# Top-k attention and SwiGLU on one core: scores and V of two units at a time, and the top-k mask applied after Exp

## The chip, the cores and the metric

The kernel runs on one core of a Trainium2 chip. The metric is the time of one execution on the device in microseconds (us). The core has a matrix engine (PE, with its weight loads shown as PEld), a Vector engine (DVE), a Scalar engine (ACT), GpSimd (POOL) and a queue that issues DMAs (SP). They work side by side, each through its own instructions in order, and wait for each other through semaphores.

## The reference

```
# q, k, v: (B=8, H=8, S=576, D=64), all float32
scores = q @ k^T / sqrt(D)
kth    = the 32nd largest score of each row
scores = where(scores >= kth, scores, -1e9)
attn   = exp(scores - max) / (sum + 1e-9)
x      = (attn @ v), brought to (B*S = 4608, H*D = 512)

# FFN: w_gate, w_val (512, 1536), w_out (1536, 512)
g   = x @ w_gate
out = (g * sigmoid(g) * (x @ w_val)) @ w_out        # (4608, 512)
```

## The kernel before, in words

**Attention.** The work is cut into 160 units, `units`: a batch, a query tile (four of 128 queries, a fifth, `qt == J`, of 64) and a pair of heads `hp`. A full unit has both heads side by side: `sc` and `e` hold 128 x 1152 elements, 576 keys for each head. A unit of the fifth tile has the two heads' 64 queries in the two halves of the partitions, and so only 576 columns. The keys are cut into four chunks of 128 (`JP` = 512 keys) and a last one of 64.

One unit goes through these functions:

- `scores(n)` (L308, and L294 for the fifth tile): Q times K into four PSUM tiles of 288 columns (two for the fifth tile). The 64 rows of each head stand in one half of the array's rows, so that two products run side by side in a tiling written 64\*128 in the trace. ACT copies the results to `sc` (L313, L299).
- `select(n)`: DVE finds the 32 largest of each row by four MAX8 (L328), with three MATCH_REPLACE8 between them (L332) that take the found ones out. Then one TENSOR_SCALAR (L338) makes from `sc` the penalty `(sc < kth) * -3e38` in `e`.
- `penalize(n)`: POOL multiplies the largest by the scale for Exp's bias (L348) and adds `sc` to the penalty (L350).
- `weigh(n)`: ACT takes Exp of `e`, with its sum in `tot` (L359, the sum is read by an instruction of its own), and adds eps (L364).
- `normalize(n)`: DVE takes the reciprocal of `tot` (L371), ACT scales `e` by it (L374).
- `turn(n)`: PE transposes `e` in chunks (L386), ACT copies them to `et` (L387).
- `values(n)`: V times `et`. The last keys of both heads stand in one 128 x 128 tile, `vl`, whose other quarters are zero (L406, the whole array, 128\*128); the four other chunks go by pairs of 64 columns, one for each head, side by side (L415, 128\*64). ACT copies the result into `xT`, the FFN's input (L430).

`fetch` (L263, L255) transposes the Q and K of the next batch's head pairs.

**FFN.** 18 blocks of 256 tokens. `feed(kb)` makes the instructions of a block in pieces: 12 products of `x` with a slice of the two weights (L470), each of two pieces of four matmuls; ACT and POOL work on each (gate: L495, L496, L497 and the product L498; value: L502 and L503); then the output product, for all blocks but the first by seven products of quarters (L556) with sums on POOL. A block can start when all its V results are in `xT`; eight units make a block and some of the next.

**Order.** The program writes the order of each engine by hand. The loop at the end has one turn for each unit, and in turn n it puts, each on its engine's queue:

```python
penalize(n - 1); flush(on_pool); run(scaled)     # scaled: unit n - 2's scaling on ACT
finish_unit(n - 3)                               # V
run(nxt); weigh(n - 1)                           # nxt: scores(n + 1)
dve(2); pieces(2); dve(1); dve(1)                # top-k of unit n
run(turn(n - 2)); pieces(1); dve(1); pieces(1); dve(2)
run(topk); next(norm); pieces(6)                 # rest of top-k, reciprocal of n - 1
```

`dve(k)` puts k steps of top-k for each head on DVE; `pieces(k)` puts up to k FFN pieces as long as `credit` allows. What ACT and POOL have to do for the pieces is kept in `on_act` and `on_pool` and put in their queues by `flush`. `share(n)` gives the credit of a turn: 7.0 (6.4 after the first block) pieces for a full unit, half for the fifth tile, less what the turn's scores (0.7), transposes (0.6) and V (0.7) take. In the last four turns it is 8. What is left runs after the loop. `weights()` rounds the FFN's weights during the first turns (L114 to L123).

PSUM has eight banks: five for `ps_t` (scores, transposes, V) and three for `ps_f` (FFN). `sc` and `e` have three buffers each, `et` two.

Of the kernel before, what the change touches and what calls it, by code (L numbers as in the profile page):

```python
# [9 lines left out]
ALU = mybir.AluOpType  # L10
# [15 lines left out]
def kernel(  # L26
# [66 lines left out]
    for i in range(NV):  # L93
        vt = consts.tile([P, P], FP32, name=f"vlast{i}")
        nc.vector.memset(vt[:], 0.0)
        vlast.append(vt)
    eps = consts.tile([P, 1], FP32, name="eps")
    nc.vector.memset(eps[:], EPS)
    wg = consts.tile([P, KC, DFF], FP32, name="wg")
    wv = consts.tile([P, KC, DFF], FP32, name="wv")  # L100
    wo = consts.tile([P, MC, DM], FP32, name="wo")
# [130 lines left out]
    def load_v(i):  # L232
        b, hp = pairs[i]
        h = slice(2 * hp, 2 * hp + 2)
        vt = slabs.tile([P, 2, J, D], FP32, tag="v", name="v")
        v_last = slabs.tile([R, 2, D], FP32, tag="vl", name="v_last")
        vl = vlast[i % NV]
        nc.sync.dma_start(
            vt[:].rearrange("p h j d -> p h (j d)"),
            v[b, h, 0:JP].rearrange("h (p j) d -> p h (j d)", j=J),  # L240
        )
        nc.sync.dma_start(v_last[:], v[b, h, JP:S].rearrange("h p d -> p h d"))
        for hh in range(2):
            o = hh * R
            nc.sync.dma_start(vl[o : o + R, o : o + R], v[b, 2 * hp + hh, JP:S])
        vs[i] = (vt, v_last, vl)
# [27 lines left out]
    def n_heads(qt):  # L274

        return 1 if qt == J else 2
# [39 lines left out]
    def select(n):  # L316

        nh = n_heads(units[n][1])
        sc = state[n]["sc"]
        m = small.tile([P, 2, TOP_K], FP32, tag="m", name="m", bufs=2)  # L320
        heads = [slice(t * S, (t + 1) * S) for t in range(nh)]
        e = work.tile([P, 2 * S], FP32, tag="e", name="e", bufs=3)
        state[n] |= dict(m=m, e=e, heads=heads)
        cur = sc
        rounds = TOP_K // 8
        for r in range(rounds):
            for t, hs in enumerate(heads):
                nc.vector.max(m[:, t, 8 * r : 8 * r + 8], cur[:, hs])  # L328
                yield
            if r < rounds - 1:  # L330
                for t, hs in enumerate(heads):
                    nc.vector.match_replace(  # L332
                        e[:, hs], m[:, t, 8 * r : 8 * r + 8], cur[:, hs], LOWEST
                    )
                    yield
                cur = e
        for t, hs in enumerate(heads):
            nc.vector.tensor_scalar(  # L338
                e[:, hs], sc[:, hs], m[:, t, TOP_K - 1 : TOP_K], FAR, ALU.is_lt, ALU.mult
            )  # L340

    def penalize(n):

        st = state[n]
        sc, m, e, heads = st.pop("sc"), st.pop("m"), st["e"], st["heads"]
        nh = len(heads)
        bias = small.tile([P, 2], FP32, tag="bias", name="bias")
        nc.gpsimd.tensor_scalar_mul(bias[:, 0:nh], m[:, 0:nh, 0], -scale)  # L348
        every = slice(0, nh * S)
        nc.gpsimd.tensor_tensor(e[:, every], e[:, every], sc[:, every], ALU.add)  # L350
        st["bias"] = bias

    def weigh(n):

        st = state[n]
        e, heads, bias = st["e"], st["heads"], st.pop("bias")
        tot = small.tile([P, 2], FP32, tag="tot", name="tot")
        for t, hs in enumerate(heads):
            nc.scalar.activation(  # L359
                e[:, hs], e[:, hs], AF.Exp, bias=bias[:, t : t + 1], scale=scale,  # L360
                accum_out=tot[:, t : t + 1],
            )
        nh = len(heads)
        nc.scalar.activation(tot[:, 0:nh], tot[:, 0:nh], AF.Identity, bias=eps[:])  # L364
        st["tot"] = tot

    def normalize(n):
        st = state[n]
        tot, e, heads = st.pop("tot"), st["e"], st.pop("heads")
        nh = len(heads)  # L370
        nc.vector.reciprocal(tot[:, 0:nh], tot[:, 0:nh])  # L371
        yield
        for t, hs in enumerate(heads):
            nc.scalar.mul(e[:, hs], e[:, hs], tot[:, t : t + 1])  # L374

# [18 lines left out]

    xT, done = {}, {}

    def values(n):

        b, qt, hp = units[n]
        vt, v_last, vl = vs[b * NHP + hp]  # L400
        et = state.pop(n)["et"]
        last = qt == J
        ql = R if last else P
        av = ps_t.tile([P, P], FP32, tag="t", name="av")
        if not last:
            nc.tensor.matmul(av[:], vl[:], et[:, J, :], start=True, stop=False)  # L406
        for c in range(J + 1 if last else J):
            kl = R if c == J else P
            for hh in range(2):
                moving = (  # L410
                    et[0:kl, c, hh * R : (hh + 1) * R]
                    if last
                    else et[:, c + hh * (J + 1), :]
                )
                nc.tensor.matmul(  # L415
                    av[hh * R : (hh + 1) * R, 0:ql],
                    v_last[:, hh, :] if c == J else vt[:, hh, c, :],
                    moving,
                    start=last and c == 0,
                    stop=c == (J if last else J - 1),  # L420
                )
        c0 = b * S + qt * P
        at = c0
        while at < c0 + ql:
            kb = at // BLK
            n_c = min((kb + 1) * BLK, c0 + ql) - at
            if kb not in xT:
                xT[kb] = ffn.tile([P, NHP, BLK], FP32, tag="xT", name="xT", bufs=3)
                done[kb] = 0
            nc.scalar.copy(  # L430
                xT[kb][:, hp, at - kb * BLK : at - kb * BLK + n_c],
                av[:, at - c0 : at - c0 + n_c],
            )
            done[kb] += n_c
            at += n_c

    def store(o, g0, cols=slice(0, DM), queues=(nc.sync,)):
# [241 lines left out]
    def fetch(n):  # L679

        b, qt, hp = units[n]
        i = b * NHP + hp
        if qt == 0:
            yield from prep(i)
        if qt == J and i + NHP < len(pairs):
            load(i + NHP)

    def share(n):


        others = 0.0
        for m, cost in ((n + 1, 0.7), (n - TURN, 0.6), (n - VALUES, 0.7)):
            if m >= 0:
                others += cost * (0.5 if units[m][1] == J else 1)
        if units[n + 2][1] == 0:
            others += 0.6

        beside = 6.4 if T[1] else 7.0
        return beside * n_heads(units[n][1]) / 2 - others

    def pieces(n):
        for _ in range(n):
            if credit[0] >= 1:
                credit[0] -= piece()

    def run(steps):
        for _ in steps:
            pass

    def finish_unit(n):  # L710
        values(n)
        b, qt, hp = units[n]
        if qt == J and b + 1 < B:
            load_v((b + 1) * NHP + hp)

    load(0)
    rounding(2)
# [2 lines left out]
    run(scores(0))  # L720
    early[0]()
    run(fetch(1))
    credit = [0.0]
    no = iter(())
    scaled = no
    TURN, VALUES = 2, 3
    due = [2.0]
    for n in range(NU + VALUES):
        nh = n_heads(units[n][1]) if n < NU else 1
        topk = select(n) if n < NU else no  # L730
        norm = normalize(n - 1) if 0 <= n - 1 < NU else no
        nxt = scores(n + 1) if n + 1 < NU else no
        ahead = fetch(n + 2) if n + 2 < NU else no

        def dve(k, beside=True):

            for _ in range(k * nh):
                next(topk, None)
                due[0] += 5 / 6 if beside else 0
                if due[0] >= 1:  # L740
                    due[0] -= 1
                    rounding(1)

        if n >= NU - NHP:
            credit[0] = 8.0
        else:
            credit[0] = min(credit[0] + share(n), share(n) + 1)
        flush(on_act)
        if 0 <= n - 1 < NU:
            penalize(n - 1)  # L750
        flush(on_pool)
        run(scaled)
        if n >= VALUES:
            finish_unit(n - VALUES)
        run(nxt)
        early[0]()
        if 0 <= n - 1 < NU:
            weigh(n - 1)


        dve(2, beside=False)
        if 2 <= n + 2 < NHP:
            load(n + 2)
        if n < NHP:
            load_v(n)
        pieces(2)
        flush(on_act)
        dve(1)
        dve(1)
        if 0 <= n - TURN < NU:  # L770
            run(turn(n - TURN))

        flush(on_pool)
        next(ahead, None)
        pieces(1)
        next(ahead, None)
        dve(1)
        pieces(1)
        dve(2, beside=False)
        run(topk)  # L780
        next(norm, None)
        scaled = norm
        pieces(6)
    while piece():
        pass
# [48 lines left out]
```

## Time and profile before

| what | us |
|---|---|
| median of 10 runs | 1810.04 (1806.59 to 1812.60) |
| the profiled execution | 1811.92 |
| its span, first to last instruction | 1809.9 |
| PE busy | 1706.0 |
| DVE busy | 1616.7 |
| ACT busy | 1220.9 |
| POOL busy | 1038.8 |
| last mask of top-k on DVE (L338) starts at | 1717.9 |

The busy times are of the whole span. A matmul's length in the trace has its way through the array in it, so lengths overlap: what a matmul costs is read from the start of one to the start of the next. The PE clock that the throttle granted was 0.65 in the mean of the first 130 us and 1.00 from 200 to 1666 us.

### The profile page before, as it was taken

Reading aid. Unit: us, or ns where it says so; the run is one execution under the profiler, and the core shown is the slowest. Engines: PE = TensorE matmul, PEld = TensorE weight load, DVE = VectorE, ACT = ScalarE, POOL = GpSimd, SP = SyncE. Lnnn points to the kernel's source line nnn. Section 1 sums busy time; section 2 is a strip of 40 time slices with the busy share of each in tenths; the row PEclk is TensorE's granted clock in tenths of the full one; section 3 lists DMA queues with packets and bytes.
Section 4 is the critical chain, followed back from the end, with each engine's and each line's share of the span. In section 5 each row is a group of like instructions: output and inputs, shape, how many; then the busy total and the mean of one; then the engine's idle time right before and its main releaser. Section 6 shows DMA issues by size and latency. Waiting matters only on the chain.

```text
span 1809.9 us, 30379 instructions
## 1 busy us (share of the span) xinstructions
PE 1706.0 (94%) x10756; PEld 1403.6 (78%) x10756; DVE 1616.7 (89%) x3372; ACT 1220.9 (67%) x2977; POOL 1038.8 (57%) x930
## 2 busy tenths in 40 slices
PE   4559999899999999999999999999999999999999
PEld 2337678687888778887888878888888878888877
DVE  7999999999999989998999989998999979999400
ACT  6778776676767676767766676766776667676522
POOL 5778666455564646564555646655556544646434
PEclk7659999999999999999999999999999999999989
DMA  7433030001200020000200021000300011000000
GB/s 190 127 103 96 21 86 1 12 2 44 50 12 2 14 71 11 13 1 24 71 13 1 14 60 34 1 12 3 92 1 13 1 40 29 13 1 13 1 12 12
DMA packets 109304, 59.64 MB, mean 33 GB/s; under 512 B 88544, under 2 KB 96992, under 8 KB 109152
## 3 DMA queue, kind: packets, MB, share of 16 engines
q1 hardware_dynamic: 108016, 57.37, 12.2%
q8 instruction: 85, 1.39, 0.3%
q14 instruction: 67, 0.55, 0.1%
q10 hardware_dynamic: 1136, 0.33, 0.1%
HBM read 48.23 MB, written 9.44 MB: 32 GB/s over the span
## 4 chain that ended last, share of the span: by engine, by line
PE 83%; DVE 7%; ACT 6%; POOL 2%; issue 0%; DMA 0%; SPq 0%; ACTq 0%; POOLq 0%
PE f L470 40%; PE x_ps L556 9%; PE av L415 8%; PE s L308 8%; PE y_ps L556 7%; PE etps L386 6%; DVE m L328 3%; DVE e L332 3%; PE s L294 2%; PE av L406 2%; ACT et L387 1%; PE o_ps L516 1%; ACT e L359 1%; DVE e L338 1%; DVE size L121 1%; ACT kqT L268 1%
## 5 line engine op out<-in xcount | busy, mean ns | idle before, releaser
L328 DVE MAX8 m<-e 128x8 f32<-128x576 f32 x864 | 614.3, 746 | 3.3
L350 POOL TENSOR_TENSOR e<-e,sc 128x1152 f32<-128x1152 f32 (+1 forms) x160 | 383.0, 2394 | 86.9 <-DVE tot L371 70.9
L332 DVE MATCH_REPLACE8 e<-m,e 128x576 f32<-128x576 f32 x576 | 423.2, 740 | 0.0
L470 PE MATMUL f<-xT,wg 128*128 128x256 f32 x1728 | 407.2, 384 | 0.9 <-ACT xT L430 0.9
L470 PE MATMUL f<-xT,wv 128*128 128x256 f32 x1728 | 403.4, 382 | 0.0
L470 PEld LDWEIGHTS f<-xT,wg 128*128 128x128 f32 x1728 | 322.2, 191 | 61.7 <-issue 20.1
L470 PEld LDWEIGHTS f<-xT,wv 128*128 128x128 f32 x1728 | 320.6, 190 | 59.6 <-issue 19.9
L498 POOL TENSOR_TENSOR h<-h,half_g 128x512 f32<-128x512 f32 x108 | 137.7, 1275 | 286.0 <-ACT h L497 268.3
L503 POOL TENSOR_TENSOR h<-h,val 128x512 f32<-128x512 f32 x108 | 139.5, 1291 | 190.8 <-ACT val L502 190.5
L359 ACT ACTIVATE e<-e,bias 128x576 f32<-128x576 f32 x288 | 224.7, 795 | 26.6 <-POOL e L350 26.5
L374 ACT ACTIVATE e<-e,tot 128x576 f32<-128x576 f32 x288 | 210.1, 776 | 28.1 <-DVE tot L371 28.1
L387 ACT COPY et<-etps 128x512 f32<-128x512 f32 (+1 forms) x448 | 182.3, 480 | 53.6 <-PE etps L386 52.8
L332 DVE MATCH_REPLACE8 e<-m,sc 128x576 f32<-128x576 f32 x288 | 211.6, 740 | 0.0
L328 DVE MAX8 m<-sc 128x8 f32<-128x576 f32 x288 | 202.5, 739 | 9.2 <-ACT sc L313 9.2
L386 PE MATMUL etps<-ident,e 128*128 128x128 f32 (+1 forms) x1312 | 174.5, 278 | 18.6 <-ACT xT L430 12.8
L386 PEld LDWEIGHTS etps<-ident,e 128*128 128x128 f32 (+1 forms) x1312 | 155.0, 143 | 42.7 <-issue 25.1
L313 ACT COPY sc<-s 128x288 f32<-128x288 f32 x512 | 167.7, 417 | 27.4 <-PE s L308 26.2
L308 PE MATMUL s<-kqT 64*128 64x288 f32 x1024 | 172.0, 457 | 13.5 <-ACT kqT L268 12.7
L338 DVE TENSOR_SCALAR e<-sc,m 128x576 f32<-128x576 f32 x288 | 179.4, 659 | 1.1
L415 PE MATMUL av<-et,v 128*64 128x128 f32 (+1 forms) x2560 | 173.4, 280 | 6.9 <-ACT et L387 6.9
L415 PEld LDWEIGHTS av<-et,v 128*64 128x64 f32 x2560 | 136.1, 143 | 32.0 <-ACT et L387 9.3
L495 ACT ACTIVATE h<-f 128x512 f32<-128x512 f32 x108 | 64.1, 593 | 128.3 <-PE f L470 128.3
(73 smaller groups left out, 2043.9 us busy)
## 6 DMA issues: line engine op xcount, KB each, us to landing
v<-in_v_dram SPq DMA_DIRECT2D x32, 256.0 KB, 3.0
kq_in<-in_k_dram SPq DMA_DIRECT2D x63, 128.0 KB, 2.9
kq_in<-in_q_dram SPq DMA_DIRECT2D x63, 128.0 KB, 3.0
w<-in_moe_w_gate_dram SPq DMA_DIRECT2D x12, 512.0 KB, 3.7
w<-in_moe_w_val_dram SPq DMA_DIRECT2D x12, 512.0 KB, 3.7
w<-in_moe_w_out_dram SPq DMA_DIRECT2D x12, 512.0 KB, 3.6
out_dram<-o SPq DMA_DIRECT2D x38, 128.0 KB, 2.4
out_dram<-o SPq DMA_DIRECT2D x16, 256.0 KB, 2.4
```

The costliest lines, as they stand in the source:

```text
L308: nc.tensor.matmul(ps[:, 0:half], slab[d, q0 : q0 + P], slab[d, k0 : k0 + half])
L328: nc.vector.max(m[:, t, 8 * r : 8 * r + 8], cur[:, hs])
L332: nc.vector.match_replace(e[:, hs], m[:, t, 8 * r : 8 * r + 8], cur[:, hs], LOWEST)
L338: nc.vector.tensor_scalar(e[:, hs], sc[:, hs], m[:, t, TOP_K - 1 : TOP_K], FAR, ALU.is_lt, ALU.mult)
L350: nc.gpsimd.tensor_tensor(e[:, every], e[:, every], sc[:, every], ALU.add)
L359: nc.scalar.activation(e[:, hs], e[:, hs], AF.Exp, bias=bias[:, t : t + 1], scale=scale, accum_out=tot[:, t : t + 1],)
L374: nc.scalar.mul(e[:, hs], e[:, hs], tot[:, t : t + 1])
L386: nc.tensor.transpose(ps[0:kl, c * P : (c + 1) * P], e[:, k0 : k0 + kl], ident[:])
L387: nc.scalar.copy(et[0:kl, c0 : c0 + cn, :], ps[0:kl, 0 : cn * P].rearrange("p (c j) -> p c j", c=cn),)
L415: nc.tensor.matmul(av[hh * R : (hh + 1) * R, 0:ql], v_last[:, hh, :] if c == J else vt[:, hh, c, :], moving, start=last and c == 0, stop=c ...
L470: nc.tensor.matmul(ps[:, i, :], w[:, kc, m * P : (m + 1) * P], x[:, kc, :], start=(kc == 0), stop=(kc == KC - 1),)
L556: nc.tensor.matmul(ps, lhsT, T[i][m], start=m == 0, stop=m == MQ - 1)
```

## The change

- **V of two units in one go.** `values` takes two neighbouring units (two head pairs of one query tile) and puts their results in one PSUM tile of 128 x 2 x 128; one ACT copy takes both. In odd turns n it works on units n-3 and n-2; in even turns there is none.
- **Scores of two units in odd turns.** In an odd turn n, scores(n+1) come first, then V of the two units, then the matmuls of scores(n+2); their copies on ACT stand behind Exp and scaling. `share` counts these costs where they now are.
- **Last keys in column pairs.** The tile `vl` is used in two halves of 64 columns, in the tiling of the other chunks, ahead of them.
- **Exp of the bare scores.** MATCH_REPLACE8 writes to a tile of its own, `rest`. In turn n, ACT takes Exp of unit n's scores without mask (`weigh(n)`), with the bias from the first MAX8 by way of POOL, while DVE is at that unit's top-k. At the end of top-k, DVE multiplies the weights by the mask `sc >= kth` and sums them, in one scalar_tensor_tensor for each head. `penalize`, Exp's own sums and ACT's addition of eps are gone; POOL adds eps.
- **Moved.** POOL's addition of eps for unit n-1 stands near the start of turn n, the reciprocal behind the first MAX8 and MATCH_REPLACE8 of unit n, the scaling behind Exp of unit n. The transposes of unit n-1 are in turn n (before: of n-2). The first loads of Q and K and their transposes come a turn earlier (`fetch(n + 3)`).

```diff
@@ select
+        rest = work.tile([P, 2 * S], FP32, tag="rest", name="rest", bufs=1)
         e = work.tile([P, 2 * S], FP32, tag="e", name="e", bufs=3)
+        tot = small.tile([P, 2], FP32, tag="tot", name="tot")
...
-                        e[:, hs], m[:, t, 8 * r : 8 * r + 8], cur[:, hs], LOWEST
+                        rest[:, hs], m[:, t, 8 * r : 8 * r + 8], cur[:, hs], LOWEST
...
-            nc.vector.tensor_scalar(
-                e[:, hs], sc[:, hs], m[:, t, TOP_K - 1 : TOP_K], FAR, ALU.is_lt, ALU.mult
+            nc.vector.scalar_tensor_tensor(
+                e[:, hs], sc[:, hs], m[:, t, TOP_K - 1 : TOP_K], e[:, hs],
+                ALU.is_ge, ALU.mult, accum_out=tot[:, t : t + 1],
             )
@@ weigh (penalize is taken out, its bias is kept here)
         nc.gpsimd.tensor_scalar_mul(bias[:, 0:nh], m[:, 0:nh, 0], -scale)
-        every = slice(0, nh * S)
-        nc.gpsimd.tensor_tensor(e[:, every], e[:, every], sc[:, every], ALU.add)
...
             nc.scalar.activation(
-                e[:, hs], e[:, hs], AF.Exp, bias=bias[:, t : t + 1], scale=scale,
-                accum_out=tot[:, t : t + 1],
+                e[:, hs], sc[:, hs], AF.Exp, bias=bias[:, t : t + 1], scale=scale
             )
-        nc.scalar.activation(tot[:, 0:nh], tot[:, 0:nh], AF.Identity, bias=eps[:])
@@ normalize
+        nc.gpsimd.tensor_scalar_add(tot[:, 0:nh], tot[:, 0:nh], EPS)
+        yield
         nc.vector.reciprocal(tot[:, 0:nh], tot[:, 0:nh])
-        yield
@@ values
-        av = ps_t.tile([P, P], FP32, tag="t", name="av")
-        if not last:
-            nc.tensor.matmul(av[:], vl[:], et[:, J, :], start=True, stop=False)
+        av = ps_t.tile([P, 2, P], FP32, tag="t", name="av")
+        for i, n in enumerate(ns):
...
+                    if c == J:
+                        weights_, at = (v_last[:, hh, :], d) if last else (vl[:, d], None)
...
-                xT[kb][:, hp, at - kb * BLK : at - kb * BLK + n_c],
-                av[:, at - c0 : at - c0 + n_c],
+                xT[kb][:, hps, at - kb * BLK : at - kb * BLK + n_c],
+                av[:, 0 : len(ns), at - c0 : at - c0 + n_c],
@@ the turn
-        if 0 <= n - 1 < NU:
-            penalize(n - 1)
         flush(on_pool)
-        run(scaled)
-        if n >= VALUES:
-            finish_unit(n - VALUES)
-        run(nxt)
-        early[0]()
-        if 0 <= n - 1 < NU:
-            weigh(n - 1)
-        dve(2, beside=False)
+        next(norm, None)
+        if nxt:
+            run(nxt.pop(0))
+        if valued(n):
+            finish_units(valued(n))
+        if nxt:
+            next(nxt[0])
+        dve(1, beside=False)
+        if n < NU:
+            weigh(n)
+        dve(1, beside=False)
+        run(norm)
+        if nxt:
+            run(nxt.pop())
+        early[0]()
...
-        pieces(2)
+        pieces(2 + (n + 1) % 2)
...
         run(topk)
-        next(norm, None)
-        scaled = norm
         pieces(6)
```

## Prediction

> **What bounds the kernel now.** I read the page's busy times and slices first, then the stretches, the waits, the groups, and the matrix engine (PE) in order of time.
>
> ```profile
> PE 1706.0 (94%) x10756; PEld 1403.6 (78%) x10756; DVE 1616.7 (89%) x3372; ACT 1220.9 (67%) x2977; POOL 1038.8 (57%) x930
> ...
> PE   4559999899999999999999999999999999999999
> ...
> DVE  7999999999999989998999989998999979999400
> ```
>
> Two engines are nearly full. In the first three slices PE is half idle, since no FFN block has its inputs yet, and the Vector engine (DVE) works without a gap. Afterwards both are full, and in the last two slices PE works alone. The stretches give this in us (columns: length, then busy time of PE, PEld, DVE, ACT, POOL, the PE clock, DMA):
>
> ```profile
> 0.00:130.00 130.00, 65.06 (x322) 44.85 (x322) 119.72 (x249) 98.02 (x221) 87.59 (x70) 0.65 0.51 139
> 130.00:200.00 70.00, 65.58 (x374) 53.19 (x375) 70.00 (x132) 62.00 (x140) 62.62 (x48) 0.95 0.27 83
> 200.00:1666.00 1466.00, 1439.39 (x9327) 1189.40 (x9326) 1400.43 (x2940) 1010.23 (x2509) 824.08 (x746) 1.00 0.09 23
> 1666.00:1740.00 74.00, 70.33 (x422) 59.45 (x422) 25.27 (x51) 34.70 (x79) 37.81 (x41) 0.99 0.06 15
> ```
>
> From 200 to 1666 us (where DVE begins unit 156) PE idles 26.6 us and DVE 65.6: PE is the bound, DVE 4.5% behind it. ACT and POOL have room. DVE's idle time is all waiting for work behind PE:
>
> ```profile
> DVE tot L371 <- ACT tot L364: 79.7, 32, 14.4
> ...
> DVE e L332 <- PE etps L386: 25.2, 29, 2.3
> ```
>
> So a saving on PE is worth at most what DVE's idle time allows, and time added to DVE beyond that idle time lengthens the run. ACT's and POOL's savings are worth nothing by themselves.
>
> **The change on PE.** In order of time (start, length, engine, line):
>
> ```profile
> 811.47 0.38 PE L406 MATMUL av<-et,vlast 128*128 128x128 f32 x2
> 811.79 1.09 PE L415 MATMUL av<-et,v 128*64 128x128 f32 x16
> 812.81 1.24 PE L308 MATMUL s<-kqT 64*128 64x288 f32 x8
> 813.98 1.56 PE L556 MATMUL x_ps<-wo,h 128*128 128x256 f32 x6
> 815.38 1.89 PE L470 MATMUL f<-xT,wg 128*128 128x256 f32 x8
> ```
>
> Here "128*64" is the tiling of the array, and starts tell more than lengths. Undisturbed passes start 0.109 us apart at 128 columns (a pair of tiles in one such step), 0.243 at 288, 0.216 at 256. So the steps would take 0.22, 0.87, 0.97 and 1.30 us, and from start to start they take 0.32, 1.02, 1.17 and 1.40: 0.55 us more, for three changes of tiling, 0.18 each. V's last-key product costs two steps of 0.109 whether it is one full matmul or a column pair, so this edit alone is worth nothing; it keeps one tiling through both V products. Counted in the order of PE's instructions, 484 changes of tiling become 322: 162 x 0.18 = 29 us less PE work (zero if the changes only move to places where they cost double). V's product for units 6 and 7 also comes in turn 9, not 10, so FFN starts one 12.3 us turn earlier, of which PE idles some 9.
>
> **ACT and POOL.** ACT loses 288 accumulator reads and 160 additions of eps (61.9 + 37.8 + 9.4 us), and 192 copies of V results become 96 of twice the width. POOL loses the penalty (383.0 us) and gains 160 small additions at the price of its bias rows, some 40. Neither engine is on the path, so I price this at nothing; the cover is their idle time (33% and 43%). Loading two head pairs earlier adds nothing to SP's queue but order.
>
> **The change on DVE.** Its other instructions stay; the mask changes:
>
> ```profile
> L328 DVE MAX8 m<-sc 128x8 f32<-128x576 f32 x288 | 202.5, 739 | 9.2 <-ACT sc L313 9.2
> ...
> L338 DVE TENSOR_SCALAR e<-sc,m 128x576 f32<-128x576 f32 x288 | 179.4, 659 | 1.1
> ```
>
> The old mask reads one tensor. Its median length is 511 ns, its next instruction starts 0.418 us later in the median and 0.585 in the mean; the long ones (up to 2.8 us) coincide with a POOL tensor operation, so 0.167 us a head is contention with POOL. A MAX8 over the same 576 elements starts its successor after 0.66. So the old mask is a two-elements-a-cycle pass: 0.418 where one element a cycle would be 0.60 and a fixed part. The new mask reads scores and weights, masks, multiplies and sums. No row shows it. Nearest below: MAX8's 0.66. Nearest above: 0.418 + 0.30 for the other half of the elements, 0.72. I take 0.70. The sum is read out in an instruction of its own on ACT; on DVE the nearest rows are MATCH_VALUE_LOAD (0.066 from start to start) and the reciprocal (0.075 so, 0.156 long): I take 0.07. Contention I leave at 0.167: the POOL operations that collide are FFN's, which remain; the bounds are 0 and 0.25. Together 0.94 against 0.585, 0.355 more a head; bounds 0.14 (0.66 + 0.066) and 0.54 (0.72 + 0.156 + 0.25).
>
> The Trainium skill (VectorE: DVE Perf Modes, The perf-mode tier table) says that a one-tensor fp32 operation in SBUF runs at two elements a cycle and a two-tensor one at one. That is the reading above. A harsher rule speaks against the change: in Vector Engine (DVE) Microarchitecture Reference, Points that are easy to get wrong, the scalar-tensor-tensor form with two non-bf16 SBUF sources is said to halve throughput. Read as half of one element a cycle, that would add another 0.60 a head and 170 us to the sum below. No row here shows it, and the sum doesn't use it.
>
> **The moved waits.** The reciprocal of unit n-1 moves from the end of DVE's turn n to behind its first four operations, 2.8 us in (1.4 in the half turns with 64 queries). It now waits for POOL's addition of eps, queued behind an FFN product that waits for ACT: gate 1.6 us (L495 to L497), POOL product 1.28, addition 0.25, some 3.3 us with hand-overs after PE's last product. Behind it on DVE stands the rest of top-k; for it waits ACT's scaling, then PE's transposes of the same turn, with two or three FFN pieces (1.73 us each) as cover. In turns 1 to 14, where DVE was the bound, PE began its turn up to 4.4 us ahead of DVE; with a lead of 1 to 2 us full turns don't wait, and half turns wait about 0.5: 32 x 0.5 = 15 us.
>
> **The sum.** Units 0 to 155 hold 284 heads. DVE up to unit 156: first wait 10.3 + busy 1590.1 (119.7 + 70.0 + 1400.4) + 284 x 0.355 = 100.8 + stalls 15 = 1716, where it was 1666; the old idle time, 65.6, is used up. From there PE's backlog decides: it began that turn at 1671.5 and took 138.4 us to the end; by the order of instructions 7.0 us of FFN come earlier, and tiling saves 1: 130. Span 1846, plus 2.0 around it (1811.92 - 1809.9), less 1.9 (the profiled run above the median): **1846 us**, slower by 2.0%. PE's idle time up to there grows by the 50 us of DVE, and by 29 - 7 of its own.
>
> **Rivals.** *The new mask is cheap* (other side): if POOL doesn't hold it up and overheads are least, 0.14 a head is 40 us, and the sum gives 1785. PE's floor lies below: 1809.9 - 29 - 9 = 1772. The point of decision is 64 us, 0.23 a head. For it: POOL has 340 us less work. Against: the old penalty began after the mask it followed, so it never stood in that mask's way. *The short chain stalls every turn*: if PE lags as in the middle of the run (its turn began 4 to 6 us after DVE's), the reciprocal waits in full turns too; 0.5 us in each of 128 more gives 64 us, 1910. Against: with DVE longer, PE gets ahead. *The tiling gain doesn't come*: with DVE the bound it costs nothing, 1847.
>
> **Chances.** DVE the bound, 1818 to 1885: 0.58 (the third rival in it). Cheap mask: 0.25 faster, and 0.05 close to even. Stalls, or a mask at its upper bound (1898): 0.12. The range 1785 to 1895 leaves out parts of the first and last rival; the likeliest case alone is 1818 to 1885. About 0.2% (3.6 us) is what a measurement can tell here: faster 0.25, same 0.05, slower 0.70.
>
> **What would show it.** Right: DVE over 95% busy from 200 us on, the mask with its sum 0.85 us a head or more, PE idling some 70 us more before unit 156, 162 fewer gaps at tiling changes, PE alone for 65 us at the end. Wrong: a mask with successors under 0.80 us later; DVE idle before the reciprocal in most turns; PE without gaps.

## The result, and the profile after

The changed kernel takes **1880.86 us** in the median of 8 runs (1875.95 to 1884.17), the kernel before 1809.62 in the median of 28: the ratio is 1.039, 95% interval 1.038 to 1.040, so 71 us slower. 1846 was predicted. The profiled execution took 1876.91 us, its span is 1875.1.

From the page after (busy times, two of the slices, the chain's shares by engine):

```profile
PE 1706.2 (91%) x11012; PEld 1388.3 (74%) x11012; DVE 1723.8 (92%) x3659; ACT 1135.4 (61%) x2433; POOL 721.2 (38%) x930
...
PE   4458999798999999999999999999999999899989
...
DVE  7999999998999999999999999999999999999520
...
DVE 47%; PE 32%; issue 7%; ACT 6%; POOL 6%; DMA 1%; SPq 1%; DVEq 0%; POOLq 0%; ACTq 0%
```

DVE has 107 us more work than before, ACT 86 less and POOL 318 less. The chain that ended last runs through DVE for 47%; in the kernel before it was PE's:

```profile
PE 83%; DVE 7%; ACT 6%; POOL 2%; issue 0%; DMA 0%; SPq 0%; ACTq 0%; POOLq 0%
```

In tenths both rows are eights and nines nearly throughout; the stretches tell the engines apart (columns as before; unit 156 now begins at 1746 us):

```profile
0.00:130.00 130.00, 61.58 (x356) 43.01 (x356) 116.80 (x252) 91.81 (x189) 62.09 (x68) 0.67 0.51 136
130.00:200.00 70.00, 63.09 (x360) 52.26 (x361) 66.12 (x132) 58.13 (x118) 48.89 (x44) 0.95 0.27 88
200.00:1746.00 1546.00, 1461.01 (x9649) 1190.14 (x9648) 1512.88 (x3223) 947.00 (x2054) 555.92 (x755) 0.99 0.09 22
```

From 200 us to unit 156 DVE is busy 97.9% of the time and PE 94.5%: they have changed places. The new mask in the groups (busy time, mean ns of one, idle before):

```profile
L338 DVE SCALAR_TENSOR_TENSOR e<-sc,m,e 128x576 f32<-128x576 f32 x288 | 291.4, 1043 | 4.3
```

and, in the groups by form, the read-out of its sum:

```profile
L338 DVE DVE_READ_ACCUMULATOR e<-sc,m,e 128x1 f32 x288 | 22.8, 79 | 0.0
```

The old mask's row had 659 ns in the mean. In order of time (start, length, engine), one unit's two masks:

```profile
1292.84 0.82 DVE L338 SCALAR_TENSOR_TENSOR e<-sc,m,e 128x576 f32<-128x576 f32 x1
1293.02 1.77 POOL L493 TENSOR_TENSOR h<-h,half_g 128x512 f32<-128x512 f32 x1 [2.38 <-ACT h L492]
1293.57 0.10 DVE L338 DVE_READ_ACCUMULATOR e<-sc,m,e 128x1 f32 x1
1293.57 1.84 DVE L338 SCALAR_TENSOR_TENSOR e<-sc,m,e 128x576 f32<-128x576 f32 x1
...
1296.88 0.22 POOL L359 TENSOR_SCALAR tot<-tot 128x2 f32<-128x2 f32 x1
...
1298.11 0.15 DVE L361 RECIPROCAL tot<-tot 128x2 f32<-128x2 f32 x1
```

The first mask's successor starts 0.73 us after it, together with the read-out of the sum, which so costs nothing. The second starts while POOL works on an FFN product and takes 1.84. Eps (L359) stands behind that product and the next. Last, what DVE waited for up to unit 156, in the changed kernel (us in total, times, longest):

```profile
DVE tot L361 <- POOL tot L359: 28.2, 20, 4.2
DVE m L328 <- ACT sc L311: 9.2, 1, 9.2
DVE size L119 <- ACT size L112: 3.1, 2, 2.5
DVE vlast L95 <- PEq L828: 0.8, 1, 0.8
```

and the two larger waits of the kernel before, up to its unit 156 (the prediction shows them for the whole span):

```profile
DVE tot L371 <- ACT tot L364: 38.2, 27, 6.7
DVE e L332 <- PE etps L386: 19.6, 26, 2.3
```

The prediction's sum beside what came of it, in us. Busy and idle are DVE's up to its start of unit 156; a mask's cost is from its start to the start of the next instruction.

| term | before | predicted | after |
|---|---|---|---|
| DVE busy | 1590.5 | +100.8 | 1695.6 (+105.1) |
| DVE idle | 75.8 | 25.3 | 50.2 |
| unit 156 begins | 1666.3 | 1716 | 1745.8 |
| from there to the end | 143.6 | 130 | 129.3 |
| mask, per head, mean | 0.585 | 0.94 | 0.972 |
| PE idle up to there | 96.0 | +72 | 160.3 (+64) |

### The profile page after: what moved, and what is told of

Read it like the earlier page. It is cut to its first block, busy times and chain, and to the rows that moved or that the text cites. A ratio compares the mean times of both kernels' runs of the same rounds, so it can differ in the third digit from the quotient of the medians.

```text
span 1875.1 us, 30744 instructions
## 1 busy us (share of the span) xinstructions
PE 1706.2 (91%) x11012; PEld 1388.3 (74%) x11012; DVE 1723.8 (92%) x3659; ACT 1135.4 (61%) x2433; POOL 721.2 (38%) x930
## 4 chain that ended last, share of the span: by engine, by line
DVE 47%; PE 32%; issue 7%; ACT 6%; POOL 6%; DMA 1%; SPq 1%; DVEq 0%; POOLq 0%; ACTq 0%
DVE m L328 21%; DVE rest L332 19%; PE f L465 14%; DVE e L338 6%; PE x_ps L551 4%; PE av L409 3%; PE etps L375 3%; PE y_ps L551 3%; ACT e L351 2%; PE s L306 2%; ACT e L363 1%; POOL h L599 1%; POOL p L537 1%; PE s L292 1%; PE o_ps L511 1%
## 5 line engine op out<-in xcount | busy, mean ns | idle before, releaser
L328 DVE MAX8 m<-rest 128x8 f32<-128x576 f32 x864 | 612.8, 744 | 2.2
L332 DVE MATCH_REPLACE8 rest<-m,rest 128x576 f32<-128x576 f32 x576 | 423.3, 740 | 0.0
L351 ACT ACTIVATE e<-sc,bias 128x576 f32<-128x576 f32 x288 | 209.7, 772 | 263.8 <-POOL bias L349 263.4
L375 PE MATMUL etps<-ident,e 128*128 128x128 f32 (+1 forms) x1312 | 194.8, 287 | 127.8 <-ACT e L363 125.8
L338 DVE SCALAR_TENSOR_TENSOR e<-sc,m,e 128x576 f32<-128x576 f32 x288 | 291.4, 1043 | 4.3
L493 POOL TENSOR_TENSOR h<-h,half_g 128x512 f32<-128x512 f32 x108 | 147.9, 1370 | 358.9 <-ACT h L492 357.8
L332 DVE MATCH_REPLACE8 rest<-m,sc 128x576 f32<-128x576 f32 x288 | 211.4, 739 | 0.0
L311 ACT COPY sc<-s 128x288 f32<-128x288 f32 x512 | 165.9, 411 | 62.0 <-PE s L306 61.2
L409 PE MATMUL av<-et,v 128*64 128x128 f32 (+1 forms) x2560 | 158.5, 267 | 0.0
L306 PEld LDWEIGHTS s<-kqT 64*128 64x128 f32 x1024 | 96.7, 194 | 65.7 <-issue 24.8
L359 POOL TENSOR_SCALAR tot<-tot 128x2 f32<-128x2 f32 (+1 forms) x160 | 35.3, 221 | 225.2 <-DVE e L338 219.0
```

The lines of the kernel that those rows point to most:

```text
L306: nc.tensor.matmul(ps[:, 0:half], slab[d, q0 : q0 + P], slab[d, k0 : k0 + half])
L311: nc.scalar.copy(sc[:, i * half : (i + 1) * half], ps[:, 0:half])
L332: nc.vector.match_replace(rest[:, hs], m[:, t, 8 * r : 8 * r + 8], cur[:, hs], LOWEST)
L338: nc.vector.scalar_tensor_tensor(e[:, hs], sc[:, hs], m[:, t, TOP_K - 1 : TOP_K], e[:, hs], ALU.is_ge, ALU.mult, accum_out=tot[:, t : t + 1],)
L351: nc.scalar.activation(e[:, hs], sc[:, hs], AF.Exp, bias=bias[:, t : t + 1], scale=scale)
L375: nc.tensor.transpose(ps[0:kl, c * P : (c + 1) * P], e[:, k0 : k0 + kl], ident[:])
```

## The experiments

The theory: DVE has become the bound; the mask's second tensor and DVE's wait through POOL's eps make the whole loss, and the pairs are a gain of their own. Its rivals put the loss on the pairing, on the chain that Exp now waits for, or on POOL's work. "Changed kernel" is the kernel after.

### The two halves of the change

**pairs_alone.** The kernel before, with scores and V of two units (in even turns, so that its longer softmax keeps its place) and the last keys in column pairs:

```diff
+        ahead = [] if n % 2 else [n + 1, n + 2]
...
+        behind = [] if n % 2 else [n - 4, n - 3]
...
-        pieces(2)
+        pieces(2 + n % 2)
```

> The first half of the change by itself: scores and V of two units in every second turn, last keys of V in column pairs, one copy for both V results; the softmax is as before (penalty on DVE, addition on POOL, masked Exp with its sum on ACT). Theory (PE loses some 29 us of tiling changes, and was the bound before): DVE's busy time up to unit 156 stays at 1590 us, its idle time there falls from 76 us to under 55, and the time falls to 1780 to 1795 us. Rival (the gain on PE is hidden or eaten by waits for PSUM banks): 1805 to 1815 us, with new gaps of PE ahead of the scores.

Measured: 1792.42 us, ratio 0.991 (0.989 to 0.992). Its stretches show where:

```profile
0.00:130.00 130.00, 60.47 (x313) 42.61 (x314) 115.88 (x242) 96.75 (x215) 85.14 (x68) 0.65 0.51 139
130.00:200.00 70.00, 62.82 (x382) 51.34 (x382) 70.00 (x130) 58.58 (x128) 61.26 (x46) 0.92 0.27 83
200.00:1650.00 1450.00, 1428.46 (x9572) 1187.28 (x9571) 1415.05 (x2949) 1001.99 (x2439) 831.27 (x750) 0.99 0.09 24
1650.00:1789.00 139.00, 131.86 (x750) 113.28 (x748) 26.57 (x54) 48.15 (x100) 63.97 (x68) 0.99 0.05 11
```

By starts in the trace, PE's changes of tiling fall from 576 to 431, and PE's busy time from 1706.0 to 1683.6: 0.15 us for each change. DVE's idle time to unit 156 falls from 75.8 to 49.1. From 200 us to 1650 us PE is busy 98.5% of the time and DVE 97.6%: with PE as the bound, the tiling gain comes.

**exp_single.** The changed kernel, with one unit's scores and V in each turn (the last keys stay in column pairs):

```diff
-        ahead = [n + 1, n + 2] if n % 2 else [] if n else [1]
+        ahead = [n + 1]
-        behind = [n - 3, n - 2] if n % 2 else []
+        behind = [n - 2]
-        pieces(2 + (n + 1) % 2)
+        pieces(2)
```

> The second half by itself: the changed kernel with scores(n+1) and V of unit n-2 in every turn instead of pairs in every second turn (so 3 changes of tiling in each turn, as before the change). Theory (DVE is the bound, PE has room): within 12 us of the changed kernel, 1870 to 1893 us, PE's idle time some 29 us shorter. Rival (PE still counts): the 29 us come on top, 1905 us or more.

Measured: 1857.64 us, ratio 1.027 (1.025 to 1.028). A miss: the theory said that pairs cost or bring little once DVE is the bound. Undoing them makes the changed kernel 23 us faster, though PE has its 577 changes of tiling again. DVE's idle time is 39.7 instead of 50.2 (its wait for eps 19.1 instead of 28.2), its busy time 6.5 lower. So pairing is worth 17 us beside the old softmax, where pairs_alone adds it, and costs 23 beside the new.

### The mask

**cheap_mask.** The changed kernel with a one-tensor mask. It leaves out the product of mask and weights and their sum (`tot` is a copy of one column of the maxima):

```diff
-            nc.vector.scalar_tensor_tensor(
-                e[:, hs], sc[:, hs], m[:, t, TOP_K - 1 : TOP_K], e[:, hs],
-                ALU.is_ge, ALU.mult, accum_out=tot[:, t : t + 1],
-            )
+            nc.vector.tensor_scalar(
+                e[:, hs], e[:, hs], m[:, t, TOP_K - 1 : TOP_K], 1.0, ALU.is_ge, ALU.mult
+            )
+            nc.vector.tensor_copy(tot[:, t : t + 1], m[:, t, 0:1])
```

> The changed kernel, all in its place, but the mask reads one tensor only (tensor_scalar on the weights) and the sum is replaced by a one-column copy, so the weights aren't multiplied by the mask and the sum is left out. Theory (the two-tensor pass on DVE is the cost): a head costs about 0.66 us instead of 0.97, DVE's busy time up to unit 156 falls by some 90 us to about 1605, and the time to 1785 to 1810 us. Rival (the moved waits are the cost): DVE's idle time grows by what its busy time loses, and the time stays above 1850 us.

Measured: 1821.97 us, ratio 1.007 (1.005 to 1.009), 59 us less than the changed kernel, but above the expected range. DVE's busy time to unit 156 falls by 83 as expected; its idle time rises from 50.2 to 75.4. The wait that grows is the one for eps, up to unit 156 (28.2 us in 20 waits in the changed kernel):

```profile
DVE tot L361 <- POOL tot L359: 50.6, 35, 5.6
```

So a part of what the mask saves is given back in the other term.

**mask_alone.** The disputed cost by itself: only masks on DVE over 128x576, alone and beside a queue of POOL operations over 128x512; everything else is left out. Edit: a kernel of its own, run once, whose core is in short

```python
nc.vector.scalar_tensor_tensor(e, sc, kth, e, ALU.is_ge, ALU.mult, accum_out=tot)  # L67; L72 without sum
nc.vector.tensor_scalar(e, sc, kth, FAR, ALU.is_lt, ALU.mult)                      # L76
nc.gpsimd.tensor_tensor(h, h, g, ALU.mult)                                         # L82
```

> Only masks on DVE (128 x 576, 20 in a row in each stretch) and products on POOL (128 x 512), apart and beside each other; nothing of the reference is computed. Theory (a two-tensor pass is one element a cycle, and both kinds of mask are held up by whole POOL operations): alone, the mask with sum and the two-tensor mask without sum start their successors after 0.72 to 0.75 us each (the sum costs under 0.03), the one-tensor mask after 0.42; beside POOL products of two tensors, every mask waits for whole products, so that both kinds take some 1.3 to 2 us each. Rival (only the two-tensor mask meets POOL, in part): the one-tensor mask keeps 0.42 beside POOL, or the two share the port and both slow down by less than a whole product.

From its timeline (rows of the same kind are drawn together, xcount):

```profile
11.05 0.81 DVE L67 SCALAR_TENSOR_TENSOR e<-sc,kth,e 128x576 f32<-128x576 f32 x1
11.78 0.08 DVE L67 DVE_READ_ACCUMULATOR e<-sc,kth,e 128x1 f32 x1
11.78 0.81 DVE L67 SCALAR_TENSOR_TENSOR e<-sc,kth,e 128x576 f32<-128x576 f32 x1
...
26.68 14.66 DVE L72 SCALAR_TENSOR_TENSOR e<-sc,kth,e 128x576 f32<-128x576 f32 x20
...
42.10 8.66 DVE L76 TENSOR_SCALAR e<-sc,kth 128x576 f32<-128x576 f32 x20
...
51.38 12.24 POOL L82 TENSOR_TENSOR h<-h,g 128x512 f32<-128x512 f32 x10
...
64.34 34.23 POOL L82 TENSOR_TENSOR h<-h,g 128x512 f32<-128x512 f32 x20
...
66.15 1.80 DVE L67 SCALAR_TENSOR_TENSOR e<-sc,kth,e 128x576 f32<-128x576 f32 x1
67.88 0.08 DVE L67 DVE_READ_ACCUMULATOR e<-sc,kth,e 128x1 f32 x1
67.88 1.80 DVE L67 SCALAR_TENSOR_TENSOR e<-sc,kth,e 128x576 f32<-128x576 f32 x1
```

Alone, a mask with two tensors takes 0.73 to 0.74 us from start to start, with its sum or without (14.66 / 20), one with one tensor 0.43 (8.66 / 20). Beside POOL's products, mask and product take turns: a mask 1.73 instead of 0.74, a product 1.71 instead of 1.22. The one-tensor mask goes from 0.43 to 1.44 there, the same 1.0 more. In the last stretch, beside a POOL operation over 128x512 that reads one tensor, the two-tensor mask is held up only every other time (1.08 and 0.74). So POOL's products hold up either kind of mask alike when they get in first.

How often that happens can be counted in the whole kernels. When a mask starts, a POOL operation on tensors is under way at 85 of 288 masks before, 104 in pairs_alone, 107 in cheap_mask and 114 in the changed kernel; the masks' lengths, above the shortest one of each kernel, sum to 48.0, 61.9, 61.5 and 73.8 us. The first three have a short mask: about half of the rise comes with the new places of the work in time, the pairs alone being enough for it, and only the other half goes with the longer mask.

**short_products.** The changed kernel with FFN's two products on POOL cut to one column of each half; the rest of the gate is left out:

```diff
-nc.gpsimd.tensor_mul(h[:], h[:], half[:])
+nc.gpsimd.tensor_mul(h[:, :, 0:1], h[:, :, 0:1], half[:, :, 0:1])
-nc.gpsimd.tensor_mul(h[:], h[:], val[:])
+nc.gpsimd.tensor_mul(h[:, :, 0:1], h[:, :, 0:1], val[:, :, 0:1])
```

> The changed kernel with FFN's two products on POOL cut to one column in each half (the rest of the gate and value products is left out), everything else in place, eps too. Theory (POOL's products hold up the mask at the port, and stand ahead of eps): mean start-to-start time of a mask falls from 0.97 to 0.85 us, DVE's busy time up to unit 156 by 30 to 40 us to about 1660, its idle time below 35 us, the time to 1815 to 1838 us. Rival (only the place in POOL's queue matters): the mask keeps 0.95 or more and the time is as without eps, 1841 us.

Measured: 1826.67 us, ratio 1.009 (1.008 to 1.011), 54 us off. The mask's spacing falls to 0.828 in the mean (its lengths above the shortest sum to 32.6 us), DVE's busy time by 43.4, its wait for eps from 28.2 to 18.2. So the products cost through both terms, mostly through the mask's. Idle time, 42.2 us, stays above the expected 35: of the wait that is left 8.4 us still stand behind these products, though they take only 0.2 us now, because the products themselves wait for ACT, and 8.8 us behind the output product's differences (L599). What eps waits for is its place in POOL's queue more than the length of a product.

### The chain behind the top-k

**no_eps.** The changed kernel without POOL's addition of eps, so that the reciprocal follows DVE's own sum. 1e-9 is left out of a sum that is 1 or more:

```diff
-        nc.gpsimd.tensor_scalar_add(tot[:, 0:nh], tot[:, 0:nh], EPS)
```

> The changed kernel without POOL's addition of eps to the sum (1e-9, left out), so that the reciprocal waits for no POOL instruction. Theory (of DVE's 50 us idle time up to unit 156 some 27 are reciprocals that wait for POOL): that idle time falls to about 25 us and the time by 15 to 27 us, to 1853 to 1866 us. Rival (the same wait comes back at the mask, through Exp's bias on POOL): the idle time moves to the mask and the time stays within 6 us of 1881.

Measured: 1841.19 us, ratio 1.017 (1.016 to 1.019): 40 us for 160 additions of 0.22 us on an engine that is busy 38% of the time, more than expected. DVE's largest waits up to unit 156 now are:

```profile
DVE m L328 <- ACT sc L311: 9.0, 1, 9.0
DVE size L119 <- ACT size L112: 4.8, 3, 1.6
DVE e L338 <- ACT e L351: 2.8, 2, 1.9
```

The reciprocal no longer stands in the list, and idle time falls from 50.2 to 28.7. The rest is in DVE's busy time, 12.0 lower (the mask's mean falls to 0.93), 2.5 us at the end, and some 4 us by which the median of the changed kernel lies above its profiled execution.

**no_pool_chain.** no_eps, and Exp without subtracting the row's largest score, so that it doesn't wait for POOL's bias:

```diff
-        bias = small.tile([P, 2], FP32, tag="bias", name="bias")
-        nc.gpsimd.tensor_scalar_mul(bias[:, 0:nh], m[:, 0:nh, 0], -scale)
...
-                e[:, hs], sc[:, hs], AF.Exp, bias=bias[:, t : t + 1], scale=scale
+                e[:, hs], sc[:, hs], AF.Exp, scale=scale
```

> The changed kernel without the addition of eps and without the subtraction of the row's largest score in Exp (both left out), so that no POOL instruction stands between top-k, Exp, the reciprocal and the transposes. Theory (what is left of the loss without eps, 1841 us, is DVE's mask of 0.97 us a head and some stalls): DVE's busy time up to unit 156 stays at 1680 to 1690 us, its idle time falls from 29 to 10 to 18 us, PE's waits for scaled weights fall from 95 to below 60 us, the time is 1822 to 1838 us, still above the kernel before. Rival (the waits through POOL are the main cost): the time falls below 1812 us.

Measured: 1841.77 us, ratio 1.018 (1.016 to 1.019), the same as no_eps: a miss. DVE's idle time is 26.0 us, not 10 to 18, and PE's wait for scaled weights rose from 101.9 to 111.3 us over the whole span. Without eps, the longest wait of ACT was not on the path. In the waits of the changed kernel it reads:

```profile
ACT e L351 <- POOL bias L349: 263.4, 89, 6.2
```

and in those of no_pool_chain ACT waits for the reciprocal instead:

```profile
ACT e L360 <- DVE tot L358: 205.6, 74, 6.3
```

**single_no_eps.** exp_single and no_eps together.

```diff
-        ahead = [n + 1, n + 2] if n % 2 else [] if n else [1]
+        ahead = [n + 1]
...
-        nc.gpsimd.tensor_scalar_add(tot[:, 0:nh], tot[:, 0:nh], EPS)
```

> Scores and V of one unit in every turn with the new softmax, without the addition of eps. It asks why pairs cost 23 us beside the new softmax (1881 against 1858) and gain 17 beside the old. Theory (in pairs the even turns have little PE work ahead of the transposes, and there the chain through eps is waited for): without eps the difference to pairs (1841) falls under 8 us, so 1833 to 1845 us. Rival (the pairs cost by themselves, through PSUM or ACT's order): the 23 us remain, 1815 to 1822 us.

Measured: 1830.33 us, ratio 1.013 (1.010 to 1.015), between the two. Without eps the pairs cost 11 us instead of 23, so half of their cost goes through the wait for eps. Of the other 11, by the two profiles, 6 are DVE's idle time, most of it before the rounding of weights, 1 its busy time and 4 lie behind the start of unit 156; why pairs bring them about is open.

**cheap_no_eps.** cheap_mask and no_eps together (leaves out what each leaves out).

```diff
+                e[:, hs], e[:, hs], m[:, t, TOP_K - 1 : TOP_K], 1.0, ALU.is_ge, ALU.mult
...
-        nc.gpsimd.tensor_scalar_add(tot[:, 0:nh], tot[:, 0:nh], EPS)
```

> The changed kernel with both suspected costs taken away: the one-tensor mask with a one-column copy for the sum (weights not masked, sum left out) and no addition of eps. Theory (the loss is the mask's second tensor, 59 us as cheap_mask showed, and the wait for POOL's eps, 40 us as no_eps showed, and they add up): 1775 to 1795 us, about pairs alone (1792), with DVE's busy time up to unit 156 near 1605 us and its idle time under 55 us. Rival (what one frees, the other takes): 1805 us or more.

Measured: 1785.01 us, ratio 0.986 (0.985 to 0.988). The two effects add up: 96 us against 59 + 40. It lies 7 us below pairs_alone, so to within these 7 us what the changed kernel loses beside its first half is these two things. DVE idles 57.2 us, a little over the expected 55: 21.4 of them now are masks that wait for Exp. PE idles 96.6 us up to unit 156, as in the kernel before (96.0).

### Versions that were meant to be faster

**pairs_no_eps.** pairs_alone without ACT's 160 additions of eps.

```diff
-        nc.scalar.activation(tot[:, 0:nh], tot[:, 0:nh], AF.Identity, bias=eps[:])
```

> Pairs of units with the old softmax, without ACT's addition of eps to the sum (left out). Theory (PE is the bound again, ACT has room): within 6 us of pairs alone, 1786 to 1795 us. Rival (the wait of the reciprocal for ACT, 50 us in all, holds DVE and through it PE): 1770 to 1784 us.

Measured: 1789.85 us, ratio 0.989 (0.988 to 0.991), 1.1% below the kernel before and 4.8% below the changed one. Eps is worth 2.6 us here, no more than the runs of one kernel differ, and 40 in the changed kernel: with ACT, it stands in the queue just behind the sum, with no FFN product ahead of it. A second reason isn't ruled out: PE is the bound here and DVE there, and no run puts ACT's eps beside the new softmax.

**pairs_act_mask.** pairs_alone, where ACT makes the penalty (Relu of 2^100 times the distance to the 32nd score, which POOL subtracts), and DVE only scales two columns:

```diff
-            nc.vector.tensor_scalar(
-                e[:, hs], sc[:, hs], m[:, t, TOP_K - 1 : TOP_K], FAR, ALU.is_lt, ALU.mult
-            )
+        nc.vector.tensor_scalar_mul(low[:, 0:nh], m[:, 0:nh, TOP_K - 1], BIG)
...
+            nc.scalar.activation(
+                e[:, hs], sc[:, hs], AF.Relu, bias=low[:, t : t + 1], scale=-BIG
+            )
```

> Pairs of units with the old softmax, but the penalty is made by ACT (Relu of a large multiple of kth - score) and subtracted on POOL; DVE only multiplies kth, one 128 x 2 instruction a unit. The computation is the whole reference. Theory (with the mask gone DVE falls below 1450 us busy and only PE's work and the DVE-bound first ten turns count): 1755 to 1785 us, DVE idle over 100 us more. Rival (ACT with some 1420 us busy is late with PSUM copies and the chain to Exp is 2 us longer): 1795 us or more, with PE waiting for ACT.

Measured: 1865.72 us, ratio 1.030 (1.029 to 1.032). The rival holds. DVE's work falls to 1529.3 us, not below 1450, and the chain from top-k to the transposes now goes twice through ACT (waits of the whole span):

```profile
POOL e L359 <- ACT e L347: 350.1, 117, 7.2
...
DVE tot L380 <- ACT tot L373: 144.5, 66, 14.2
...
DVE e L333 <- PE etps L395: 83.9, 57, 3.0
```

The granted clock was also lower than in pairs_alone, 0.955 to 0.959 against 0.964 to 0.968; how much of the 73 us that makes was not separated.

**pairs_more.** pairs_no_eps with more credit in a turn:

```diff
-        beside = 6.4 if T[1] else 7.0
+        beside = 6.7 if T[1] else 7.3
```

> Pairs alone without eps and with 0.3 more pieces of FFN credit a turn (7.3 and 6.7). Theory (from 200 us on PE idles 21 us and DVE 34, so the middle is balanced; work drawn forward shortens the part behind unit 156 but lengthens the turns): within 5 us of 1790. Rival (the credit holds PE back): 1775 to 1784 us.

Measured: 1816.26 us, ratio 1.003 (1.002 to 1.004), 26 us slower than pairs_no_eps: a miss. DVE's two larger waits grow up to unit 156, from 14.2 and 11.5 us in pairs_no_eps to:

```profile
DVE e L332 <- PE etps L385: 36.0, 24, 2.4
DVE tot L370 <- ACT e L359: 26.1, 10, 5.1
```

PE's busy time is also 18 us longer with the same instructions. The granted clock goes with it: 0.955 to 0.959 in these six runs, 0.962 to 0.968 in those of pairs_no_eps; in the profiles the lower clock takes away as much as 80.4 us of full speed, instead of 58.0, which is 22 us more. Why the clock was lower isn't settled, nor how much of the 26 us is the credit's own. pairs_alone stays the fastest kernel that computes everything, pairs_no_eps the fastest that leaves out eps alone.

## Why the prediction was right, and where its sizes were off

**The mechanism held.** DVE, made busier than its idle time could take, became the bound, at 97.9% against the 95% asked for. The mask costs 0.972 a head against 0.85 or more. Changes of tiling fell by 144 instead of 162 (the trace has 576 and 432, where the prediction counted 484 and 322). The rival of a cheap mask failed: cheap_mask shows what it would have been worth, 59 us. But the loss is twice the one forecast, 71 us against 36, near the upper end of the likeliest case.

**Luck in two signs.** PE idles 64 us more against 70, by two errors that cancel. DVE began unit 156 79.5 us later instead of 50; and PE's own work up to there, which was to shrink by 22 us, grew by 15.1. In the whole span PE's busy time didn't fall by 29 us: it is 1706.2 after 1706.0. Counting each matmul from the end of the one before where they overlap, V's products take 28 us less and the transposes 30 us more; they take as much in exp_single, so that this comes with the new softmax, for a reason that no run shows. And DVE waits 61.2 us for PE's last products, against 65 us of PE alone, but the kernel before had the same wait, so this sign tells nothing:

```profile
DVE o L620 <- PE y_ps L556: 61.7, 1, 61.7
```

**The mask's terms.** The two-tensor pass was put at 0.70 and is 0.73 or 0.74; the sum's read-out was put at 0.07 and adds 0.01 at most; contention was put at 0.167, "the POOL operations that collide are FFN's, which remain", and rose to about 0.23, since the masks are hit more often, about half of it with the old short mask too (pairs_alone, cheap_mask). Together 0.032 a head too little, 9 us over 284 heads, because the terms cancel in part; DVE's busy time missed by 4 only.

On the two rules of the Trainium skill: VectorE: DVE Perf Modes (The perf-mode tier table) has a one-tensor fp32 operation at twice the rate of a two-tensor one, and mask_alone agrees, 0.43 against 0.74: the difference of 0.31 is what half of the elements cost, and some 0.12 is common to both. The harsher reading of Vector Engine (DVE) Microarchitecture Reference (Points that are easy to get wrong) falls: there is no further halving, with a sum or without. The Trainium skill, SBUF — State Buffer (Who interferes with whom), says that a DVE instruction with two SBUF inputs contends with a GpSimd instruction that reads SBUF, and that DVE's two-port mode contends with GpSimd too; the 1.0 us that both kinds of mask lose beside POOL's product agrees.

**The step that failed is the stalls.** "Half turns wait about 0.5: 32 x 0.5 = 15 us" gave DVE 25.3 us of idle time with its first wait, where 50.2 came (32 x 0.5 is 16, but that is the least of it). Three things were missing. The reciprocal's wait was 28.2 us, more than half of it in full turns (15.7 of 26.8 us in turns 12 to 155), which the prediction had put at zero by PE's lead. So the rival of stalls came true in part, in 20 turns of some 155. In each of them eps starts within 0.1 us of the end of another POOL operation: 12 waits (14.0 us) behind a gate or value product, as the prediction reckoned, but 5 (12.1 us, the two longest among them) behind the output product's differences (L599), which it left out, and 3 behind others. The rounding of weights waited 3.1. And some 9 us are gaps too short for the waits view, which the sum took as used up although the kernel before had 8 of them too, so that not all of its idle time was waiting behind PE; the whole kernels among the experiments have between 7.8 and 8.8, pairs_act_mask 13.4 (50.2 less the four waits shown for the changed kernel is 8.9). These 25 us and the mask's 4 are the whole of the 29 by which the span missed. The other 6 us of the 35: the median lies 4 above the profiled execution here, and lay 2 below it before. The profiled execution and the shortest of the 8 runs have the highest granted clock, 0.965 and 0.964; the others have 0.958 to 0.961.

**What lay behind it.** The price of the wait through POOL was reckoned as DVE's idle time alone. no_eps shows that it was worth 40 us, of which 21.5 are idle time of DVE and 12 busy time. And "the tiling gain doesn't come ... costs nothing, 1847" was wrong in its price: exp_single, without that gain, is 23 us faster. It is the pairing that costs this, about half of it through the same wait, and not the tiling.

**Right as priced at nothing, or close to it.** ACT's and POOL's work was taken off engines with room. The nearest comparison is cheap_no_eps with pairs_no_eps, both with a short mask and without eps: POOL has 388 us less work there and ACT 27, and the time is 5 us less. ACT's wait for the bias, 263 us in the changed kernel, cost nothing where it was taken away beside eps (no_pool_chain); by itself it was not tried.

## What to carry to other kernels

An operation is priced by the passes that it makes on the engine that it lands on, and by how often another engine's work on the same memory will meet it; work taken off engines with room paid for almost none of that here. When a small operation is handed to an engine with room, ask what stands ahead of it in that engine's queue: additions of 0.22 us in a queue of FFN work, 160 of them, cost 40 us of the run here, and 2.6, within the spread of the runs, on ACT in pairs_alone, where nothing stood ahead (but there PE was the bound). A gain on one engine (the pairs, 17 us) need not hold once another is the bound, and is worth trying alone.

## What the runs showed of the hardware that was not expected

- Reading out the sum of a two-tensor DVE operation starts together with the next instruction and adds at most 0.01 us, though it has a row of 79 ns.
- A DVE mask over 128x576 and a POOL product over 128x512 that run against each other take turns, and each is longer by a good part of the other: 1.73 and 1.71 us instead of 0.74 and 1.22.
- DVE's one-tensor and two-tensor masks lose the same time to such a product, 1.0 us.
- ACT's idle third could not be used for the mask in this order of work: 186 us more of work on ACT went with 73 us more time (pairs_act_mask against pairs_alone), at a lower granted clock.
